# Two loads for the first half of x, LN1 sums shared out anew, and more transposes ahead of K, in a DiT block

## Chip, cores, metric

One core of a Trainium2 chip. The metric is the device time of one execution in microseconds, as the median of several runs; most runs of one kernel agree within 0.3%. Changes within 2% count as the same. TensorE runs the matmuls, VectorE, ScalarE and GpSimd the elementwise work, SyncE issues the loads.

## The reference

```python
B, N, D = 2, 256, 1152          # 512 tokens = 4 tiles of 128, two for each batch; 2 heads
mod = (silu(c) @ w_mod).reshape(B, 6, 1, D)      # shift_a, scale_a, gate_a, shift_m, scale_m, gate_m
h   = layernorm(x) * (1 + scale_a) + shift_a     # "LN1" below is this layernorm
q, k, v = h @ wqkv
a   = softmax(q k^T / sqrt(Dh)) v @ wo
x   = x + gate_a * a
h2  = layernorm(x) * (1 + scale_m) + shift_m
out = x + gate_m * (gelu(h2 @ w_fc1) @ w_fc2)    # all in bfloat16
```

## The kernel before

The kernel is a list of operations with dependencies. TensorE's and SyncE's order is the program's, the first part of VectorE's and ScalarE's is given in a list, and semaphores are set where an operation reads what another engine wrote. All weights pass once through one queue of loads. What the change touches is the first 20 us:

```python
# loads, in the order of SyncE's queue
for b in range(2):
    dma(X[:, 2*b:2*b+2, :], xv[b], ...)                  # x: tiles 0,1 then 2,3; 590 KB each, 4608 B a partition
for (ka, kb) in ((0, KC), (KC, KT)):                     # KC = 4, KT = 9
    for k0, k1 in ((0, 3), (3, 6), (6, 9)):
        dma(WSC[:, k0:k1, ka*P:kb*P], wmod_v[...], ...)  # scale_a's weights, 3 loads for each group of columns
    for kt in range(ka, kb):
        dma(WK[:, kt, :], wqkv_v[:, kt, D:2*D], ...)
...
# LN1: tiles 1, 2 by bn_stats on VectorE; tiles 0, 3 by two summing activations on ScalarE;
# the power -0.5 on GpSimd; xn_t = (x - mean) * rstd on VectorE
if t in (1, 2): ln_stats_dve(...)
else:           ln_stats_act(...)
...
# TensorE ahead of K (xn_T: nine 128x128 transposes of a tile, sca: two-column scale matmuls,
# warm: matmuls that only keep the clock up, hk: the scaled tile that K needs)
xn_T(1); warm(1); sca(0, 3); xn_T(0); warm(1); sca(3, 6); warm(1); sca(6, 9)
hk(0, 0); sc1a(0, KC); hk(1, 0); ...
xn_T(3, 0, 8)
k_first(0); k_first(1)                                   # 8 matmuls of 256 columns each: the K projection begins
xn_T(3, 8, 9); xn_T(2)                                   # ten transposes inside K's stream
...
for kt in range(KT):
    mod_kt(WSC, kt, 0, ..., (KC, KT))                    # 45 two-column matmuls, the second group of scales
hk(KC, 0); ...
k_pair(range(KC), 2, 1)                                  # 8 matmuls that cover hk(KC, 0)
...
# at the end, ahead of the last store: waits for the older stores, then for VectorE
```

## Time and profile before

| | before |
|---|---|
| time, median of 5 runs | 244.14 us (243.77 to 244.27) |
| TensorE busy | 238.2 us of a span of 243.0 |
| K's first matmul | 11.80 us |
| tiles 2, 3 of x in place | 5.99 us |

Times of landing, of single matmuls and of single packets are taken from the trace's records of semaphores, instructions and transfers; views of the profile merge them.

### The profile page before, as it was taken

What the parts mean: (1) busy time and instruction counts of PE and PEld (TensorE: products, weight loads), DVE (VectorE), ACT (ScalarE), POOL (GpSimd) and SP (SyncE); (2) the same over time, 40 slices, a digit from 0 to 9 for tenths busy, and PEclk for the clock granted to TensorE, in tenths of its full rate; (3) what the DMA queues carried; (4) which work ended last, traced back from release to release, by engine and by line L of the source; (5) the groups of instructions that cost most, each with busy time, mean ns of one, the idle gap of its engine ahead of it and who ended that gap; (6) DMA issues with size and microseconds to landing.
All of it is one profiled execution on the core that took longest, in us unless ns stands there. A gap on an engine that the chain in (4) does not pass through costs nothing.

```text
span 243.0 us, 4065 instructions
## 1 busy us (share of the span) xinstructions
PE 238.2 (98%) x1753; PEld 148.0 (61%) x1763; DVE 120.4 (50%) x217; ACT 67.2 (28%) x136; POOL 21.5 (9%) x39
## 2 busy tenths in 40 slices
PE   7999999999999999999999999999999999999996
PEld 2698854556667666898444444444656656666575
DVE  3724379596997899789999600000022222111112
ACT  4730350345424206983233322222000000000000
POOL 1500000000021186400000000020000000000000
DMA  6999999999995999979953498011000000000000
GB/s 237 334 381 392 392 391 391 398 414 405 389 350 170 350 386 393 392 266 392 323 162 82 166 308 323 0 32 68 0 16 19 16 16 19 16 16 19 18 28 21
DMA packets 30140, 51.59 MB, mean 212 GB/s; under 512 B 1703, under 2 KB 15787, under 8 KB 30123
## 3 DMA queue, kind: packets, MB, share of 16 engines
q1 hardware_dynamic: 29680, 50.14, 57.7%
q0 software_dynamic: 416, 1.19, 1.6%
q8 instruction: 14, 0.23, 0.4%
q14 instruction: 3, 0.02, 0.0%
q10 hardware_dynamic: 27, 0.00, 0.0%
HBM read 50.14 MB, written 1.19 MB: 211 GB/s over the span
## 4 chain that ended last, share of the span: by engine, by line
PE 94%; DMA 3%; SPq 1%; issue 0%; DVE 0%
PE psum L688 93%; DMA arena<-in_w_mod_dram 3%; PE psum L691 1%; SPq L669 1%; DVE arena L805 0%; DVE arena L1268 0%; DVE arena L1269 0%
## 5 line engine op out<-in xcount | busy, mean ns | idle before, releaser
L688 PE MATMUL psum<-arena 128*128 128x384 bf16 (+12 forms) x1664 | 234.8, 307 | 2.4 <-POOL arena L711 1.5
L688 PEld LDWEIGHTS psum<-arena 128*128 128x128 bf16 (+3 forms) x1674 | 142.7, 97 | 90.6 <-issue 4.5
L1063 DVE SCALAR_TENSOR_TENSOR arena<-arena 128x1152 f32<-128x1152 bf16 x32 | 44.7, 1414 | 0.6
L1268 DVE TENSOR_TENSOR arena<-psum,arena 128x384 f32<-128x384 f32 (+3 forms) x14 | 7.0, 501 | 68.0 <-PE psum L688 68.0
L1177 ACT ACTIVATE arena<-psum 128x512 bf16<-128x512 f32 (+1 forms) x44 | 22.4, 520 | 42.7 <-PE psum L688 42.7
L683 ACT ACTIVATE arena<-psum 128x512 bf16<-128x512 f32 (+6 forms) x37 | 19.6, 550 | 38.6 <-PE psum L688 37.0
L685 DVE CAST arena<-psum 128x512 bf16<-128x512 f32 (+3 forms) x13 | 8.2, 641 | 11.4 <-PE psum L688 11.3
L669 POOL DMA_DIRECT2D dit_scratch<-arena x3 | 1.8, 617 | 115.6 <-DVE arena L685 58.8
L1145 POOL TENSOR_TENSOR arena<-arena 128x384 f32<-128x384 f32 x12 | 10.9, 914 | 11.4 <-DVE arena L1144 9.8
L1090 DVE CAST arena<-psum 72x32 bf16<-72x32 f32 x1 | 0.2, 187 | 21.3 <-PE psum L688 21.3
L739 DVE BATCH_NORM_STATS2 arena<-arena 128x6 f32<-128x384 f32 (+1 forms) x18 | 9.5, 548 | 0.1
L1150 ACT ACTIVATE arena<-arena 128x1152 bf16<-128x1152 f32 x4 | 5.3, 1344 | 11.1 <-DVE arena L1149 11.1
L1144 DVE TENSOR_TENSOR arena<-psum,arena 128x384 f32<-128x384 f32 x12 | 6.5, 552 | 1.5 <-PE psum L688 0.9
L1269 DVE TENSOR_TENSOR arena<-arena 128x384 bf16<-128x384 f32 (+3 forms) x14 | 7.0, 501 | 0.5
L691 PE MATMUL psum<-arena 128*128 128x128 bf16 (+1 forms) x89 | 7.1, 219 | 0.0
L691 PEld LDWEIGHTS psum<-arena 128*128 128x128 bf16 (+1 forms) x89 | 5.8, 98 | 2.0 <-DMA arena<-in_c_dram 0.8
L1167 ACT ACTIVATE arena<-psum,arena 128x128 bf16<-128x128 bf16 x16 | 6.0, 456 | 1.7 <-PE psum L691 1.1
L1164 DVE TENSOR_SCALAR arena<-psum,arena 128x128 bf16<-128x128 bf16 x20 | 5.4, 336 | 1.9 <-PE psum L691 1.9
L1070 DVE TENSOR_REDUCE arena<-arena 128x36 f32<-128x1152 f32 x4 | 5.4, 1346 | 0.0
L1067 DVE STREAM_TRANSPOSE arena<-arena 128x1152 f32<-128x1152 f32 x4 | 5.4, 1363 | 0.0
L993 ACT ACTIVATE arena<-psum,arena 128x256 bf16<-128x256 f32 x8 | 3.7, 473 | 1.3 <-PE psum L688 0.9
L947 ACT ACTIVATE arena<-arena 128x256 bf16<-128x256 bf16 x6 | 2.6, 498 | 3.9 <-DVE arena L941 3.9
(48 smaller groups left out, 45.8 us busy)
## 6 DMA issues: line engine op xcount, KB each, us to landing
arena<-in_w_fc_dram SPq DMA_DIRECT2D x9, 1152.0 KB, 7.5
arena<-in_w_fc_dram SPq DMA_DIRECT2D x4, 2592.0 KB, 17.4
arena<-in_wqkv_dram SPq DMA_DIRECT2D x18, 288.0 KB, 10.3
arena<-in_w_mod_dram SPq DMA_DIRECT2D x3, 1728.0 KB, 20.4
arena<-in_w_mod_dram SPq DMA_DIRECT2D x3, 864.0 KB, 13.3
arena<-in_w_mod_dram SPq DMA_DIRECT2D x9, 288.0 KB, 10.8
arena<-in_wqkv_dram SPq DMA_DIRECT2D x1, 2592.0 KB, 16.7
arena<-in_wo_dram SPq DMA_DIRECT2D x1, 2592.0 KB, 24.4
```

Of the source, the lines that this page charges most:

```text
L683: act(c_act(n), lambda e: e.activation(out=dst, in_=src, func=ACTF.Copy), [src], [dst], name)
L685: dve(c_dve_psum16(n) if psum16 else c_dve_psum32(n), lambda e: e.tensor_copy(dst, src), [src], [dst], name)
L688: S.instr(lambda e: e.matmul(o, lhsT=l, rhs=r, start=st, stop=sp, **kw), reads=[l, r], writes=[o])
L691: S.instr(lambda e: e.transpose(o, i_, idn), reads=[i_, idn], writes=[o])
L739: dve(550, lambda e, s=s, o=o: e.bn_stats(out=o, in_=s), [s], [o], "bn_%s_%d" % (tag, ci))
L1063: dve(1270, lambda e, w=w, s=s, acc=acc: e.scalar_tensor_tensor(out=acc, in0=w, scalar=s, in1=acc, op0=ALU.mult, op1=ALU.add), [w, s, acc] ...
L1144: dve(550, lambda e, o=o, ga=ga, x1c=x1c: e.tensor_tensor(out=x1c, in0=o, in1=ga, op=ALU.mult), [o, ga], [x1c], "wo_t1_%d_%d" % (t, ci))
L1145: S.op("pool", 930, lambda e, xs=xs, x1c=x1c: e.tensor_tensor(out=x1c, in0=x1c, in1=xs, op=ALU.add), reads=[x1c, xs], writes=[x1c], name=" ...
L1167: act(440, lambda e, o=o, dst=dst, s1=s1, s2=s2: e.activation(out=dst, in_=o, func=ACTF.Identity, scale=s1, bias=s2), [o, s1, s2], [dst], ...
L1177: act(c_act(ntok), lambda e: e.activation(out=dst, in_=o, func=ACTF.Gelu_apprx_tanh), [o], [dst], "gelu_%d_%d" % (f, tok0))
L1268: dve(c_dve_psum32(w), lambda e, o=o, gm=gm, t1=t1: e.tensor_tensor(out=t1, in0=o, in1=gm, op=ALU.mult), [o, gm], [t1], "fc2_t1_%d_%d" % ( ...
L1269: dve(c_dve_32(w), lambda e, t1=t1, x1c=x1c, ost=ost: e.tensor_tensor(out=ost, in0=t1, in1=x1c, op=ALU.add), [t1, x1c], [ost], "fc2_out_%d ...
```

## The change

Its intent: ScalarE can begin LN1 when half of the first load is there, all but two of the transposes come before K begins so that K's stream carries two instead of ten, and half a K pair goes between the scale sums, which would otherwise wait for their last weights once K begins earlier.

```diff
-        for b in range(2):
-            dma(X[:, 2 * b:2 * b + 2, :], xv[b], ..., "ld_x%d" % b)
+        for t in (1, 0):
+            dma(X[:, t:t + 1, :], xv[0][:, t:t + 1, :], ..., "ld_x0_%d" % t, run=2304)
+        dma(X[:, 2:4, :], xv[1], ..., "ld_x1")
...
-        for i in range(5):          # warm-ups ahead of c's transpose
+        for i in range(3):
...
-            if t in (1, 2):         # statistics on VectorE
+            if t in (0, 2):
...
-        xn_T(1); warm(1, "c"); sca(0, 3); xn_T(0); warm(1, "d"); sca(3, 6); warm(1, "e"); sca(6, 9)
+        xn_T(1); xn_T(0); xn_T_copy(0, ...)
+        sca(0, 3); warm(1, ...); sca(3, 6); warm(2, ...)
+        xn_T(3, 0, 8); sca(6, 9); xn_T(2, 0, 8)
...
-        xn_T(3, 0, 8)
         k_first(0)
+        xn_T(3, 8, 9); xn_T(2, 8, 9)
         k_first(1)
-        xn_T(3, 8, 9); xn_T(2)
...
         for kt in range(KT):
+            if kt == 6:
+                k12(0)              # first half of the pair
             mod_kt(WSC, kt, 0, "scb_%d" % kt, (KC, KT))
...
-        k_pair(range(KC), 2, 1)
+        k12(1)                      # second half
...
# last store: the waits for older stores now come after the wait for VectorE in the program
```

The lines that set the orders of VectorE and ScalarE, and a subtraction that goes from VectorE to GpSimd, are cut.

## The prediction

> **What bounds the kernel now.** I read the page's busy shares first, then the chain of work that ended last.
>
> ```profile
> PE 238.2 (98%) x1753; PEld 148.0 (61%) x1763; DVE 120.4 (50%) x217; ACT 67.2 (28%) x136; POOL 21.5 (9%) x39
> ...
> GB/s 237 334 381 392 392 391 391 398 414 405 389 350 170 350 386 393 392 266 392 323 162 82 166 308 323 0 32 68 0 16 19 16 16 19 16 16 19 18 28 21
> ...
> PE 94%; DMA 3%; SPq 1%; issue 0%; DVE 0%
> ```
>
> TensorE is busy for 98% of the 243.0 us, and the chain is TensorE for 94% of them. So there are only two places where time can go: a gap in TensorE's stream, or TensorE work moved into otherwise empty time. The gaps are at the front. The same chain in order of time, from the first wait to the K projection:
>
> ```profile
> 2.87 7.88 DMA arena<-in_w_mod_dram
> 10.75 0.05 issue
> 10.79 0.47 PE psum L688 x12
> 11.26 0.14 PE psum L691 x2
> 11.39 0.36 DVE arena L805
> 11.75 0.05 issue
> 11.80 1.92 PE psum L688 x16
> 13.72 0.56 PE psum L691 x10
> 14.28 19.14 PE psum L688 x234
> ```
>
> Up to 10.75 us it is a transfer: the third scale load (part of w_mod), on a queue whose second slice of 6.1 us already moves 334 GB/s. Then 12 two-column scale matmuls, the first scaled tile hk_0_0 on VectorE (L805), and K's first matmul at 11.80. From there to the end the starts of successive matmuls, taken from the trace, show only pauses of about 0.1 to 0.25 us [...]. So 11.80 is the number that matters: **the end is K's start plus a fixed 231.2 us of stream**, and the ten transposes at 13.55 (x10) belong to that stream.
>
> The LN1 work that has to be ready by then, in the timelines of ScalarE, GpSimd and VectorE:
>
> ```profile
> 4.57 1.16 ACT L747 ACTIVATE arena<-arena 128x1152 bf16<-128x1152 bf16 x1 [0.41 <-DMA arena<-in_x_dram]
> ...
> 8.29 1.16 ACT L749 ACTIVATE arena<-arena 128x1152 bf16<-128x1152 bf16 x1
> ```
>
> ```profile
> 7.53 0.67 POOL L751 TENSOR_TENSOR arena<-arena 128x1 f32<-128x1 f32 x1
> ...
> 10.41 0.68 POOL L743 TENSOR_TENSOR arena<-arena 128x1 f32<-128x1 f32 x1
> ```
>
> ```profile
> 10.47 0.58 DVE L760 TENSOR_SCALAR arena<-arena 128x1152 bf16<-128x1152 bf16 x1 [0.61 <-POOL arena L751]
> 11.38 0.36 DVE L805 TENSOR_SCALAR arena<-psum 128x256 bf16<-128x256 bf16 x1 [0.33 <-PE psum L691]
> 11.66 0.16 DVE L795 COPY arena<-psum 128x8 f32<-128x8 f32 x1
> 11.85 0.35 DVE L805 TENSOR_SCALAR arena<-psum,arena 128x256 bf16<-128x256 bf16 x1
> 12.12 0.57 DVE L760 TENSOR_SCALAR arena<-arena 128x1152 bf16<-128x1152 bf16 x1
> ...
> 19.81 0.29 DVE L805 TENSOR_SCALAR arena<-arena,psum 128x256 bf16<-128x256 bf16 x1 [4.37 <-PE psum L688]
> ```
>
> L760 normalizes a token tile. Tile 3 is done at 11.05, tile 2 only at 12.69, after K has begun, which is why nine of its transposes sit inside the K stream.
>
> **What the Trainium skill says.** "TensorE: Matmul & The Clock Gate", "Wait — 56ns, not 53.3ns?": back-to-back 128-column matmuls start 55.6 ns apart when warm. The trace has its transposes 56 ns apart: it agrees. The same page, "The cost: per-tile semaphore tail": completion increments serialize, fitted at 26.3 ns each. In this trace the two-column matmuls start 26.6 ns apart, but their semaphore increments arrive 34.15 ns apart: the same mechanism, a larger figure. The lag grows by 7.55 ns per small matmul. The same page, "What's actually happening": the clock starts at half rate and rises after a busy window of some 3.4 us. Here 512-column warm-ups start 427 ns apart until about 6.6 us and 215 ns later. "DMA: Bandwidth & Descriptors", "Why small descriptors are slow (HBM only)": a fixed cost per packet, so an estimate of 2% more time at 2304 B than at 4608 B. The trace: 590 KB of x in 4608 B packets follow in 1.44 us (5.99 minus 4.55), 295 KB of wk in 2304 B packets in 0.75. So two halves cost 1.50, 0.06 more.
>
> **The change part by part.**
>
> *The load of x in two.* The bytes in front of the scale loads are the same; one more issue costs the queue 0.42 us on SyncE, but the scale loads land long after their issue (2.87 to 10.75), so only the packet size counts: the third scale load lands at about 10.80. Tile 1, 295 KB, should land near 3.65 instead of 4.55 (half of the 1.9 us in which the first load's packets ran).
>
> *Warm-ups 5 to 3.* The transpose of c waited at 3.75 behind the fifth warm-up, though c landed at 3.14. It moves to about 3.3, tanh (3.97 now) to 3.52, and ScalarE can begin on tile 1 at 3.75: 0.82 earlier than the 4.57 above.
>
> *LN1.* I shift the measured rows. ScalarE: sums of tile 1 at 3.75, of tile 3 at 6.20 (2.45 per tile, as from 4.57 to 7.02), after the second half of x at about 6.1. GpSimd follows with its present distances (the power for a ScalarE tile starts 2.96 after that tile's first sum): tile 1 at 6.71 to 7.38, then tile 0 to 7.95, tile 3 at 9.16 to 9.83, tile 2 after VectorE's statistics at 10.0 to 10.6. VectorE: tile 0's statistics from 4.65 to 6.6 (six instructions, 2.0 us now), one statistic of tile 2, xn_1 at 7.41, xn_0 at 7.98, the rest of tile 2's statistics to 9.95, xn_3 at 9.90 to 10.47, xn_2 at 10.63 to 11.2.
>
> *TensorE before K.* Transposes of tiles 1 and 0 at about 8.0 and 8.55; scales 0 to 5; two warm-ups; tile 3's eight transposes when xn_3 is done, 10.5 to 10.95; scales 6 to 8 from 10.95 instead of 10.79, ending at 11.27; tile 2's eight from 11.27 to 11.72. The signal of the last scale matmul came 0.27 after its start, hk_0_0 started at once, and K 0.414 after that. The same steps: 11.24 + 0.27 + 0.02 + 0.414 = **11.95, 0.15 later than 11.80**. The eight transposes hide behind hk_0_0.
>
> *The K stream.* Two transposes instead of ten: 8 x 0.056 = **0.45 less**.
>
> *The pair around the scale sums.* Now 45 small matmuls start 18.07 to 19.24, then a pair of 8 x 0.109 = 0.87 covers hk_4_0 (19.81 above) and K goes on at 20.16, with only 0.02 idle. The signal of the last small matmul came at 19.78, 0.54 after its start, of which 45 x 7.55 ns = 0.34 is the semaphore lag. With four wide matmuls after the 30th, the lag starts afresh: 15 x 7.55 ns = 0.11, so the signal comes after 0.31. But only four matmuls (0.44) are left to cover signal plus hk_4_0 and its release (0.35): 0.31 + 0.02 + 0.35 = 0.68 against 0.03 + 0.44. **Gap 0.21, so 0.19 more than now.** What the split is meant to save, a wait for the third load of this group, is not there: it lands at 18.53, its matmuls start at 18.87, and the stream is to come only about 0.3 earlier.
>
> *The last wait.* The last store now waits for the old stores after VectorE: two of those waits stand behind the VectorE one. In the compiled order of the new one the VectorE wait is the last, on the store itself. The trace has it released at 241.35 and issued at 241.43: **0.08 less**.
>
> Sum: +0.15 - 0.45 + 0.19 - 0.08 = -0.19 us, from 244.16 to **243.97**.
>
> **The rivals.** (a) *A floor at the scale load.* If xn_3 comes 0.2 us sooner than I reckon, K's start returns to the scale load's landing: 11.80 plus 0.05. The sum is then -0.29, and without the gap at the scale sums -0.48: 243.7. More is not possible while this load's order and bytes are the same. (b) *LN1 becomes the bound.* xn_3 now stands ahead of scales 6 to 8 on TensorE, and xn_2 ahead of hk_0_0 on VectorE; each 0.1 us that GpSimd's powers (0.57 to 0.68 each, two in a row at the end) come later moves K by nearly as much. 0.3 late makes 244.3. (c) *The clock rises later.* With three warm-ups TensorE idles from 2.8 to 3.3 before c. If the busy window then closes 2 us later, 18 transposes take 107 instead of 56 ns, the ScalarE copy that frees the bank for tile 3 slides from 9.3 to 10.0, and tile 3's last transposes wait to about 11.1: 244.4. Against it: the warm-ups are continuous from 3.4 on and the rise now comes at 6.6. (d) *No gap in the K stream:* 243.8.
>
> **Range and chances.** The floor in (a) limits the gain to about half a microsecond, 0.2%; (b) and (c) together cost hardly more. Runs before lie within 0.16 us. So 243.6 to 244.4. Two per cent would be 4.9 us, more than the whole change can touch: within 2% has 0.99.
>
> **What would show it.** In the new profile: the first sum on ScalarE near 3.75 instead of 4.57; xn_3 near 9.9 and xn_2 near 10.6; K's first 256-column matmul near 11.95; only two transposes after it; the first hk with a VectorE wait on TensorE after the scale sums followed by a TensorE gap near 0.2; the last store 0.08 closer to its VectorE release. It would be wrong if K started well before 11.8, which needs the scale load to land sooner, or if a new wait of over 0.5 us appeared between 12 and 34 us.

## More of the kernel before

One view that the prediction does not show matters later: the early stretches of the kernel before. The columns are the stretch, its length, the busy time of TensorE, its weight loads, VectorE, ScalarE and GpSimd (with instructions), the clock, the busy share of the transfer engines and GB/s.

```profile
1.75:3.75 2.00, 2.00 (x6) 0.46 (x4) 0.00 (x0) 0.96 (x1) 0.00 (x0) 1.00 0.92 320
3.75:5.75 2.00, 2.00 (x8) 0.86 (x8) 1.44 (x5) 1.37 (x3) 0.00 (x0) 1.00 0.97 356
5.75:7.75 2.00, 2.00 (x9) 0.79 (x7) 1.71 (x6) 1.97 (x4) 1.25 (x4) 1.00 0.95 285
```

x comes in at 320 to 356 GB/s without a break; from 5.75 us on, when mostly the scale weights in packets of 1024 bytes follow, it is 285.

## The result, and the profile after

| | before | after |
|---|---|---|
| time, median of 5 runs | 244.14 us (243.77 to 244.27) | 245.5 us (245.11 to 245.86) |
| tiles 2, 3 of x in place | 5.99 us | 7.70 us |
| third scale load in place | 10.75 us | 11.43 us |
| K's first matmul | 11.80 us | 13.39 us |

The ratio is 1.0057 (95% interval 1.0044 to 1.0071). The time is 1.1 us above the top of my range.

From the page of the changed kernel, the busy line and the chain by engine:

```profile
PE 238.3 (98%) x1752; PEld 147.7 (61%) x1762; DVE 120.3 (49%) x216; ACT 67.1 (27%) x136; POOL 21.2 (9%) x40
...
PE 94%; DMA 2%; ACT 1%; DVE 1%; issue 0%; SPq 0%; POOL 0%; POOLq 0%
```

TensorE's work is the same; ScalarE has come into the chain, and VectorE has a larger share of it (DVE was at 0%). In order of time it reads:

```profile
1.69 6.01 DMA arena<-in_x_dram
7.70 0.02 issue
7.72 1.26 ACT arena L748 x2
8.99 0.02 issue
9.01 1.26 ACT arena L750 x2
...
10.68 0.56 POOL arena L752
11.24 0.03 issue
11.27 0.59 DVE arena L761
11.86 0.05 issue
11.90 0.62 PE psum L691 x8
12.53 0.29 PE psum L688 x12
...
12.98 0.36 DVE arena L806
13.34 0.05 issue
13.39 1.05 PE psum L688 x8
...
14.54 6.62 PE psum L688 x95
21.17 0.29 DVE arena L806
21.46 0.05 issue
21.51 13.26 PE psum L688 x144
```

The head of the chain is no longer the scale load but the load of tiles 2, 3, issued at 1.69 and there at 7.70. ScalarE's two sums of tile 3 follow (L748, L750), its power on GpSimd (L752), its normalization on VectorE (L761, 11.27), eight transposes at 11.90, and only then the last 12 scale matmuls, though their load had been there since 11.43. K begins at 13.39. The hop over VectorE at 21.17 is the gap behind the scale sums that the prediction speaks of.

The same early stretches in the changed kernel:

```profile
1.75:3.75 2.00, 2.00 (x7) 0.56 (x6) 0.28 (x2) 1.16 (x3) 0.00 (x0) 1.00 0.91 292
3.75:5.75 2.00, 2.00 (x6) 0.76 (x5) 1.37 (x4) 1.97 (x3) 0.26 (x1) 1.00 0.83 208
5.75:7.75 2.00, 1.63 (x6) 0.35 (x3) 0.59 (x4) 0.55 (x3) 1.24 (x3) 1.00 0.95 326
```

From 3.75 to 5.75 us, just when tiles 2, 3 should come, the engines moved 208 GB/s instead of 356. They were busy 83% of the time, but single packets took very long: of those that began between 3 and 9 us, 15 took over 380 ns (the longest 1439), where 178 ns is usual for 4608 bytes. In the kernel before there were 2. A load is in place when the last of its 16 engines has delivered: for tiles 2, 3 they delivered from 5.25 to 5.99 us before, from 5.51 to 7.70 after. The first engines are on time; the stalled ones make the wait.

**The account.** The two traces can be cut at four marks:

| part | predicted | before | after | difference |
|---|---|---|---|---|
| to K's first matmul | +0.15 | 11.80 | 13.39 | +1.59 |
| from there to the first shift matmul | -0.45 + 0.19 = -0.26 | 17.63 | 17.39 | -0.24 |
| from there to the last matmul | 0 | 211.00 | 211.00 | 0.00 |
| last matmul to issue of the last store | -0.08 | 1.00 | 0.92 | -0.08 |
| issue of the last store to the end | 0 | 1.57 | 1.45 | -0.12 |

The sum is 1.15, the difference of the spans (244.15 less 243.00). The last row is scatter: over all undisturbed traces it runs from 1.45 to 1.99 us with no regard to the kernel. So the rows between came out as reckoned, and the first row has to be explained.

### The profile page after: what moved, and what is told of

Same layout as the page of the kernel before. It is cut to its first block, busy times and chain, and to the rows that moved or that the text cites. A ratio compares the mean times of both kernels' runs of the same rounds, so it can differ in the third digit from the quotient of the medians.

```text
span 244.2 us, 4065 instructions
## 1 busy us (share of the span) xinstructions
PE 238.3 (98%) x1752; PEld 147.7 (61%) x1762; DVE 120.3 (49%) x216; ACT 67.1 (27%) x136; POOL 21.2 (9%) x40
## 4 chain that ended last, share of the span: by engine, by line
PE 94%; DMA 2%; ACT 1%; DVE 1%; issue 0%; SPq 0%; POOL 0%; POOLq 0%
PE psum L688 92%; DMA arena<-in_x_dram 2%; PE psum L691 2%; ACT arena L750 1%; ACT arena L748 1%; SPq L669 0%; DVE arena L806 0%; DVE arena L761 0%; POOL arena L752 0%; DVE arena L1275 0%; DVE arena L1276 0%; POOL arena L751 0%; POOLq L473 0%
## 5 line engine op out<-in xcount | busy, mean ns | idle before, releaser
L688 PE MATMUL psum<-arena 128*128 128x384 bf16 (+11 forms) x1663 | 234.9, 307 | 3.2 <-POOL arena L712 1.5
L688 PEld LDWEIGHTS psum<-arena 128*128 128x128 bf16 (+4 forms) x1673 | 142.4, 97 | 91.2 <-issue 4.4
L685 DVE CAST arena<-psum 128x512 bf16<-128x512 f32 (+3 forms) x13 | 8.2, 641 | 11.4 <-PE psum L688 11.3
L1152 POOL TENSOR_TENSOR arena<-arena 128x384 f32<-128x384 f32 x12 | 10.9, 911 | 11.2 <-DVE arena L1151 9.7
```

What stands on the lines that cost most here:

```text
L685: dve(c_dve_psum16(n) if psum16 else c_dve_psum32(n), lambda e: e.tensor_copy(dst, src), [src], [dst], name)
L688: S.instr(lambda e: e.matmul(o, lhsT=l, rhs=r, start=st, stop=sp, **kw), reads=[l, r], writes=[o])
L1152: S.op("pool", 930, lambda e, xs=xs, x1c=x1c: e.tensor_tensor(out=x1c, in0=x1c, in1=xs, op=ALU.add), reads=[x1c, xs], writes=[x1c], name=" ...
```

## The experiments

Every run has a trace. The table puts them together by the loads of x in SyncE's queue ("590" and "295" are KB); the text below tells each. "Slow" counts packets over 380 ns between 3 and 9 us.

| run | base | loads of x ahead of the weights | slow | tiles 2, 3 in place | third scale load | K | ratio to before |
|---|---|---|---|---|---|---|---|
| before | | 590, 590 | 2 | 5.99 | 10.75 | 11.80 | 1 |
| e4 | before | 590, 590 | 7 | 6.03 | 10.68 | 11.73 | 0.9995 |
| e1 | after | 590, 590 | 1 | 6.18 | 10.62 | 12.88 | 1.0021 |
| after | | 295, 295, 590 | 15 | 7.70 | 11.43 | 13.39 | 1.0057 |
| e14 | after | 295, 295, 590 | 10 | 7.48 | 10.72 | 13.16 | 1.0011 |
| e2 | before | 295, 295, 590 | 13 | 6.82 | 11.44 | 12.49 | 1.0033 |
| e5 | before | 295, 295 (by rows), 590 | 13 | 8.74 | 11.86 | 13.33 | 1.0052 |
| e6 | after | 295, 295, 590 (small packets) | 15 | 7.99 | 11.62 | 13.67 | 1.0047 |
| e3 | after | 4 x 295 | 3 | 5.82 (3), 6.76 (2) | 10.71 | 12.06 | 1.0013 |
| e7 | after | 4 x 295 | 8 | 5.94 (3), 6.68 (2) | 10.83 | 12.01 | 1.0009 |
| e15 | after | 4 x 295 | 6 | 5.82 (3), 7.08 (2) | 10.74 | 12.13 | 0.9999 |
| e8 | after | 295, 295, 295, 295 (last two by rows) | 15 | 8.19 | 11.94 | 13.94 | 1.0088 |
| e9 | after | 295, 295, 590, tiny | 8 | 6.86 | 10.71 | 12.54 | 1.0034 |
| e10 | before | 590, 590, tiny | 10 | 5.79 | 11.17 | 12.22 | 1.0015 |
| e11 | after | 295, 295, 590, weights later | 14 | 6.92 | 10.68 | 12.60 | 1.0028 |
| e12 | before | 590, 295, 295 | 7 | 5.51 (3), 6.68 (2) | 11.03 | 12.08 | 0.9987 |
| e13 | after | 295, 590; one more on ScalarE's queue | 3 | 5.49 | 9.95 | 15.72 | 1.0116 |

### Is the late landing the cause?

**e0_after_again**: the changed kernel once more, no edit.

> The changed kernel once more, for what repeats. In its trace the second half of x (tiles 2, 3) landed at 7.70 us instead of 5.99, and K started at 13.39 instead of 11.80. Theory S (splitting the load of tiles 0, 1 itself slows the load behind it) and theory E (ScalarE's earlier sum, 3.73 instead of 4.57 us, slows the load it runs beside) both expect about the same again: x landed at 7 to 8 us, 245.5 us. Theory C (chance of one profile) expects 5.9 to 6.2 us in this trace.

Measured: 245.35 to 245.77 us in its undisturbed runs, ratio 1.0045. The profiled execution was a disturbed one of 702 us, and its trace is not used. The slower time repeats; on the landing this run says nothing.

**e1_x_one_load**

```diff
-        for t in (1, 0):
-            dma(X[:, t:t + 1, :], xv[0][:, t:t + 1, :], ...)
-        dma(X[:, 2:4, :], xv[1], ...)
+        for b in range(2):
+            dma(X[:, 2 * b:2 * b + 2, :], xv[b], ...)
```

> The changed kernel with tiles 0, 1 of x in one load again. S and E: tiles 2, 3 land at about 6.0 us as in the kernel before, ScalarE's first sum starts at 4.57 as there. Then by the rows of before: ScalarE ends tile 3 at 9.55, its power at 10.65, tile 2's power at 11.3, tile 2 normalized at 11.9, its transposes to 12.4, K near 12.45: 0.65 later than before, less 0.45 for eight transposes out of the K stream, 0.08 at the end, plus 0.2 at the scale sums: about 244.45 us. C expects no difference to the changed kernel but that by ScalarE's later start.

Measured: tiles 2, 3 at 6.18 us, K at 12.88, 244.99 us, ratio 1.0021. ScalarE's timeline in this run:

```profile
4.79 1.16 ACT L747 ACTIVATE arena<-arena 128x1152 bf16<-128x1152 bf16 x1 [1.22 <-DMA arena<-in_x_dram]
...
7.24 1.15 ACT L747 ACTIVATE arena<-arena 128x1152 bf16<-128x1152 bf16 x1
```

The second sum no longer waits for a load: it follows the first tile's work. Without the split the late landing is gone, and half of the slowdown with it; the other half fits with this order of LN1 needing the early start that the split was to give: in the chain to K, LN1's steps follow each other from the landing at 4.77 us on. K is 0.43 later than I reckoned, 0.22 of it because the first load itself came at 4.77 instead of 4.55.

**e2_x_split_only**: the kernel before with the two lines of the split.

> The kernel before with nothing but the load of tiles 0, 1 split as in the change. Here VectorE takes tile 1 and ScalarE tile 0, so ScalarE starts no earlier than at about 4.45 us. S: tiles 2, 3 land late all the same, 7 to 8 us, the third scale load near 11.4 instead of 10.75, K near 12.4, about 244.8 us. E: tiles 2, 3 land at about 6.1 us, K within 0.1 of 11.80, 244.1 to 244.2 us.

Measured: tiles 2, 3 at 6.82, the third scale load at 11.44, K at 12.49, 245.4 us, ratio 1.0033. The split alone makes the kernel slower, with ScalarE starting at 4.41 us: theory E, that ScalarE's earlier work disturbs the load, fails as the whole cause. The landing itself is short of the 7 to 8 us that theory S expected; the third scale load and K are as S expected. Here another load is late too; among TensorE's waits from 8.5 to 25 us stands

```profile
PE psum L688 <- DMA arena<-in_w_mod_dram: 0.8, 2, 0.4
```

The two are the scale loads of both groups, and the stretch from K to the shift matmuls is 18.15 us instead of 17.63.

**e3_x_four_loads**

```diff
-        for t in (1, 0):
-            dma(X[:, t:t + 1, :], xv[0][:, t:t + 1, :], ...)
-        dma(X[:, 2:4, :], xv[1], ...)
+        for t in (1, 0, 3, 2):
+            dma(X[:, t:t + 1, :], xv[t // 2][:, t % 2:t % 2 + 1, :], ...)
```

> The changed kernel with tiles 3 and 2 in two loads as well, so that all of x comes in packets of 2304 bytes. If S acts through the step from 2304-byte to 4608-byte packets, both land at about the time of before (5.3 and 6.1 us) and the result is my predicted 243.9 to 244.1. If it acts through the number of loads, or if E holds, they land late, tile 2 at 7 us or later, and the time is 245 or more.

Measured: tile 3 at 5.82 us, tile 2 at 6.76, K at 12.06; 244.73 us where before is 244.57, ratio 1.0013 (0.9995 to 1.0031). That is above the 243.9 to 244.1 that I expected, 0.4 of it because the kernel before is higher on this chip too (244.57). The stretch in question, and ScalarE's two first sums:

```profile
3.75:5.75 2.00, 2.00 (x7) 0.60 (x5) 1.41 (x4) 1.97 (x3) 0.26 (x1) 1.00 0.95 329
```

```profile
3.75 1.16 ACT L747 ACTIVATE arena<-arena 128x1152 bf16<-128x1152 bf16 x1 [0.39 <-DMA arena<-in_x_dram]
...
6.20 1.15 ACT L747 ACTIVATE arena<-arena 128x1152 bf16<-128x1152 bf16 x1
```

With tile 3 in time, the sums begin at 3.75 and 6.20, to the hundredth what I had reckoned for the changed kernel, tile 3 is normalized at 9.94 (reckoned 9.90) and K begins at 12.06 (11.95). So the late landing accounts for 1.33 of the 1.59 us in the first row of the account, 0.15 was reckoned, and my steps behind the landing hold to 0.11. (Tile 2 runs close behind: its power ends at 10.93 and it is normalized at 10.96, reckoned 10.6 and 10.63, so that its eight transposes end just before K. That is the second half of rival (b).) **e15_four_loads_again** repeats it:

> The kernel with four loads of x, unchanged: its scatter. Tile 3 at 5.7 to 6.0 us, tile 2 at 6.6 to 6.9, K at 11.9 to 12.2, 244.4 to 245.0 us; a tile 3 after 6.5 us would say that the two traces so far were luck.

Measured: 5.82, 7.08 and K at 12.13; 244.63 us, ratio 0.9999. **e14_after_third** does so for the changed kernel:

> The changed kernel, unchanged: its scatter. All theories but chance: tiles 2, 3 between 6.8 and 7.8 us, K between 12.5 and 13.5, 245.1 to 245.9 us.

Measured: 7.48 and K at 13.16; its two runs were 245.46 (the profiled one) and 244.39 us, the second below what I expected. In this trace 15 of the 16 engines had delivered by 5.94 us and a single one held the load until 7.48. The late landing repeats; its size scatters.

### Does the split of the K pair cost what I said?

**e7_four_loads_pair_whole**: e3 with

```diff
-            if kt == 6:
-                k12(0)
...
-        k12(1)
+        k_pair(range(KC), 2, 1)
```

> The changed kernel with x in four loads and the K pair whole behind the 45 scale matmuls, as before the change. My account: the gap of 0.23 us behind the scale sums goes down to 0.02; K at about 12.05, the Q projection 0.2 earlier than in the kernel with four loads (33.48), near 33.28, and 0.2 us less in time: 244.5 where before is 244.57. Against it: if the wait for the third of the second scale loads comes into the gap's place, Q stays at 33.4 to 33.5 and the time at 244.7.

Measured: 17.39 us from K to the shift matmuls, the same as in e3; ratio 1.0009. The gap of 0.23 us behind the scale sums is gone (0.02 is left), but the chain shows what took its place:

```profile
8.16 10.65 DMA arena<-in_w_mod_dram
18.81 0.05 issue
18.86 2.21 PE psum L688 x30
```

The third load of the second group lands at 18.81 in this trace, and the last 15 scale matmuls wait 0.23 us for it. So in this trace the split would have traded one wait for an equal one. It is one trace, and the landing scatters: in e3 and e15 the same load was there at 18.09 and 18.14, and the 31st sum of e7 was due at 18.63, so with such a landing the whole pair would have waited for nothing. That the wait "is not there" was true of the changed kernel, where the sums come 1.1 us later and the load landed at 18.75; with K as early as I predicted it can come, and what the split costs or saves there is not shown.

The sign that I had named, an earlier Q projection (33.22 against 33.48), says nothing: the trace of e3 lacks the record of Q's first matmul. It has 1752 matmuls where e7 has 1762, and the first of Q that it has starts 325 ns after the matmul before it, which is 109 and one missing matmul of 216. The traces of before and of the changed kernel lack ten each against e4 and e14, the same kernels. So of the pauses that the prediction saw behind K, those of 0.22 us are missing records; the cause of those of 0.1 us is not shown.

### Why does the load land late?

**e4_before_again**: the kernel before, for a second trace.

> The kernel before, unchanged, for a second trace of it. In its first trace two packets behind 3 us took over 380 ns, against 15 in the changed kernel, 12 with the split alone and 3 with four loads of x. Theory C (chance) expects counts up to 10 here too; theories P and N (below) expect at most 4, tiles 2, 3 at 5.9 to 6.3 us and K at 11.7 to 12.0.

Measured: 7 slow packets (more than 4, so the count alone is a weak mark), landing at 6.03, K at 11.73. **e5_x_halves_by_rows**, in the kernel before:

```diff
-        for b in range(2):
-            dma(X[:, 2 * b:2 * b + 2, :], xv[b], ...)
+        for p0 in (0, 64):
+            dma(X[p0:p0 + 64, 0:2, :], xv[0][p0:p0 + 64], ...)
+        dma(X[:, 2:4, :], xv[1], ...)
```

> The kernel before with tiles 0, 1 of x loaded in two halves by partitions (0 to 63, 64 to 127), 4608-byte packets throughout. Theory N (three loads of x instead of two, one more issue ahead of the weights, makes the packets behind slow) expects over ten packets above 380 ns behind 3 us, tiles 2, 3 at 7 us or later, K at 12.3 or later. Theory P (a load in 4608-byte packets behind loads in 2304-byte packets does it) expects at most 4 such packets, tiles 2, 3 at about 6.1 us and the time of before, 244.2 to 244.6.

Measured: 8.74 us, K at 13.33, ratio 1.0052, with packets of 4608 bytes throughout. But here the halves are slow themselves: they land at 4.64 and 6.00 us, where the halves by tiles of the changed kernel land at 3.71 and 4.43. **e6_x1_small_packets**, in the changed kernel:

```diff
-        X = sb(O_X, 9216).rearrange("p (t d) -> p t d", t=4)
+        # the same bytes, tiles in the order 0, 2, 1, 3: tiles 2, 3 are two runs of 2304 bytes in each partition
```

> The changed kernel with the tiles of x laid out in the on-chip memory in the order 0, 2, 1, 3, so that tiles 2, 3, still one load, come in 2304-byte packets like the others. P: at most 4 slow packets, tiles 2, 3 at 6.0 to 6.7 us, K at 12.0 to 12.3, 244.4 to 244.9 us, near the kernel with four loads (244.73). N: slow as in the changed kernel, tiles 2, 3 after 7 us, 245.5 us.

Measured: 7.99 us, ratio 1.0047, with packets of 2304 bytes throughout. Theory P, a step in packet size, fails on both, and on e6 without that doubt. **e8_x1_by_rows**, in the changed kernel:

```diff
-        dma(X[:, 2:4, :], xv[1], ...)
+        for p0 in (0, 64):
+            dma(X[p0:p0 + 64, 2:4, :], xv[1][p0:p0 + 64], ...)
```

> The changed kernel with tiles 2, 3 loaded in two halves by partitions, 4608-byte packets: four loads of x of 295 KB, as in the kernel with four loads, but with the step in packet size. So far three loads of x were late four times out of four, two and four never. Theory L (a load of 590 KB behind two of 295 KB is what stalls) and theory M (three loads bad, four good, whatever their size) both expect the last of tiles 2, 3 at 6.7 us, K near 12.05 and 244.7 us. If it is late (over 7 us, K over 12.6) then the four loads owed their good time to the packets of 2304 bytes alone.

Measured: 8.19 us and K at 13.94, the worst of the landings but one, with four loads of 295 KB. M (three loads bad, four good) and L (the big third load is what stalls) both expected 6.7. But the loads by rows were slow in e5 from the first on, so a trouble of their own is not ruled out, and e8 alone does not refute M and L. **e9_tiny_fourth** and **e10_tiny_third** add to the changed kernel and to the kernel before, behind the loads of x:

```diff
+        dma(TINY, xv[0][:, 0, 0:2], P * 4, "ld_tiny")
```

> The changed kernel with a fourth load of 4 bytes for each partition behind the three of x, ahead of the weights. M, or a theory by which the time of issue of the first weight load matters (T: 2.16 us in the changed kernel, 2.64 with four loads), expects tiles 2, 3 at 6.0 to 6.5 us and K near 12.1. L expects tiles 2, 3 still after 7 us and K at 13 or later.

> The kernel before with the same load of 4 bytes for each partition behind its two of x. M and T expect what three loads showed: tiles 2, 3 (or the weights just behind) with over ten packets above 380 ns and the third scale load at 11.4 us or later instead of 10.7. L expects no difference to the kernel before: tiles 2, 3 at 6.0, the third scale load at 10.6 to 10.9 us.

Measured: e9 lies between (6.86, K at 12.54): later than M expected with four loads (6.0 to 6.5), earlier than L did (after 7). In e10 x is in time (5.79), but ten slow packets, eight of them of the weights behind, put the third scale load at 11.17 and K at 12.22. L expected none of this (10.6 to 10.9 for that load), M somewhat more (11.4 or later). **e11_weights_later**, in the changed kernel:

```diff
+        by["ld_sc0_0"].instrs[0].deps.update(by["c_half"].instrs)
```

> The changed kernel, its three loads as they are, but the first weight load is issued only after VectorE's first use of c (about 3.65 us instead of 2.16). Theory W (issuing the weights' loads while x moves is what stalls the third load of x) expects tiles 2, 3 at 5.5 to 6.2 us; the third scale load then at about 11, K near 12.2, 244.8 us or less. L and M expect tiles 2, 3 after 7 us as before, K at 13.3 or later, 245.5 us or more.

Measured: the weights are issued from 3.73 us on, the landing is at 6.92, K at 12.60. Better than the changed kernel and between what W (5.5 to 6.2) and L and M (after 7) expected, but 14 slow packets are left: the weights' issue is not all that makes them. **e12_second_split**, in the kernel before:

```diff
-            dma(X[:, 2:4, :], xv[1], ...)
+        for t in (3, 2):
+            dma(X[:, t:t + 1, :], xv[1][:, t - 2:t - 1, :], ...)
```

> The kernel before with tiles 0, 1 in one load as there and tiles 3, 2 in two: three loads of x, but the split is in the second place. Theory F (it is the split of the first load that hurts: the engines reach the third load early, while little is queued) expects tiles 2, 3 by 6.3 us, the third scale load at 10.6 to 10.9, K at 11.7 to 12.0. Theory N (any third load) expects the last of them after 6.7 us or the third scale load after 11.1, K at 12.2 or later.

Measured: 6.68 for the last tile, 11.03 for the third scale load, K at 12.08: between what F and N expect, nearer to N. The time is 244.33 against 244.68, unclear (0.996 to 1.0014). **e13_tile1_on_act_queue**, in the changed kernel:

```diff
-        for t in (1, 0):
-            dma(X[:, t:t + 1, :], ...)
+        dma(X[:, 1:2, :], xv[0][:, 1:2, :], ..., eng="act")
+        dma(X[:, 0:1, :], xv[0][:, 0:1, :], ...)
...          # the load's place in ScalarE's list, and one semaphore more
```

> The changed kernel with the load of tile 1 issued from ScalarE, behind that of c, so that SyncE's queue has two loads of x as in the kernel before. If the late landing comes from three x loads in one queue (N, F): tiles 2, 3 at 5.8 to 6.3 us, the third scale load by 10.8, K at 11.9 to 12.2, 244.0 to 244.5 us where before is 244.3. If it comes from splitting in whatever queue: tiles 2, 3 after 6.7 us, K at 12.5 or later, 244.9 us or more.

Measured: tiles 2, 3 at 5.49 us and the third scale load at 9.95, 0.8 earlier than in the kernel before, with 3 slow packets: SyncE's queue with two loads of x was in order. But tile 1, on the other queue, came only at 5.9 us, TensorE stood idle, and its clock fell:

```profile
6.47 1.92 PE L688 MATMUL psum<-arena 128*128 128x512 bf16 x6
10.60 1.95 PE L691 MATMUL psum<-arena 128*128 128x128 bf16 x18 [2.21 <-DVE arena L761]
```

The first transposes still start 55 to 69 ns apart, those from 10.85 us on 107 instead of 56. K began at 15.72, ratio 1.0116: the landing was as hoped, the time as feared for another reason. The clock is the smaller part of it: three runs had a mean clock of 0.993 and took 247.85 to 248.01 us, and the fourth, at 1.0, took 246.58, still 1.9 above the kernel before (244.68).

**What follows.** In the four traces with two loads of x in SyncE's queue and nothing more ahead of the weights (before, e4, e1, e13), tiles 2, 3 were in place by 6.2 us and the third scale load by 10.75. In every trace with more, one of the two was later: the last of x at 6.7 to 8.7 us, or (e10) the scale load. In the split that I study the loss sits in packets that take up to 1.4 us, from about 4 us on. That much is shown. Which property of the additional loads makes single packets wait is open. A step in packet size (e6), ScalarE's work beside it (e2) and the weights' issue (e11) have each failed as the sole cause; a big load behind small ones did so in e10, which has none; against the number three there are only e8, with its doubt, and e9, which lies between. Most versions have one trace, and traces of like loads (after and e14 against e2, e9, e11) scatter by 0.9 us.

None of the versions is shown to beat the kernel before: e3, e7 and e15 reach it within 0.13%, and e12's 0.9987 is within its scatter.

## Why the prediction was wrong

"Within 2%" was right; the time and the range were not. By its own steps:

- **The load of x in two: wrong, and nearly the whole error.** The step that failed reads "the scale loads land long after their issue (2.87 to 10.75), so only the packet size counts", with "the second half of x at about 6.1" by the same reckoning. I treated the queue as a pipe that moves bytes at one rate whatever they are cut into. The measured landing was 7.70, so the sum of tile 3 began at 7.72 instead of 6.20. From there to K I had 5.75 us (6.20 to 11.95); the trace has 5.67. Of the signs that I named, xn_3 (11.27 for 9.9), xn_2 (11.92 for 10.6) and K (13.39 for 11.95) show it; the landing itself I had not named.
- **The early start: right.** ScalarE began at 3.73 (reckoned 3.75), since tile 1 landed at 3.71 (3.65). But K does not hang on tile 1. The time won there ends in a wait of 1.45 us before tile 3's sum.
- **Ten transposes to two, and the gap behind the scale sums: right.** Together -0.24, reckoned -0.26. The gap was 0.23 (reckoned 0.21); hk_4_0 started 0.341 after the last scale matmul's start (reckoned 0.31 + 0.02), against 0.57 before, as the lag of the semaphore increments demands. That the split saved no wait was partly luck: it held in the changed kernel, whose K came 1.4 us later than I had it, and not in e7.
- **The last wait: right.** -0.08.
- **The rivals.** Rival (b) named the bound that came, LN1 of tile 3 ahead of the scale matmuls, but only GpSimd's powers as its reason, with 0.1 to 0.3 us. No rival let the transfer itself get slower, and so the range ended at 244.4. It was too narrow even for the rivals that I had: (b) at 0.3 us and (c), 244.4 by itself, together give 244.7. Rival (c), a clock that rises later, did not come in the changed kernel (the first warm-up at 217 ns started at 6.79 us, 6.74 before); in e13 transposes ran at 107 ns, since the clock had fallen again.
- **Was the gain real otherwise?** With tile 3 in time (e3, e15) K is 0.26 to 0.33 later than before instead of 0.15, which the -0.24 and the -0.08 just pay for.

## What to carry to other kernels

A load cut in two was not the same stream in smaller pieces here: look at the landing of the load behind it, not only at that of the first half, and give the range room for it when the chain begins with a transfer. Work moved ahead of a critical stage ties that stage to more inputs; ask for each of them what it does if it is a microsecond late. When the other terms are right to 0.1 us and the total is off by 1.5, cut the traces at a few marks before thinking about causes.

## What the Trainium skill lacked or had wrong

- "TensorE: Matmul & The Clock Gate", "The cost: per-tile semaphore tail", fits 26.3 ns for each serialized increment and 4.7 more for each tile, 31.0 where every matmul has one. Here increments of two-column matmuls arrive 34.15 ns apart while the matmuls start 26.6 ns apart; the lag, 0.34 us after 45 of them, was worth 0.2 us at a hand-over to VectorE.
- The same page, "What's actually happening", has the clock fall after an idle window of some 3.4 us. In e13 about 2.2 us without a matmul (8.39 to 10.60 us) came before it: the next four gaps were still 55 to 69 ns, those from 10.85 us on 107. The 3.4 us that ended with this fall held some 1.2 us of matmuls, an estimate from these starts and ends. The rise came between 4.8 and 7.7 us over the traces, 3.3 to 6.2 us after the first warm-up, for nearly the same stream of warm-ups.
- "DMA: Bandwidth & Descriptors" prices a transfer by its bytes, its packets and a fixed cost. No section that I found tells that one more load ahead in the same queue can slow the packets of the next: 208 GB/s instead of 356 over 2 us, packets of up to 1439 ns where 178 is usual.
- No page that I read gives the scatter of a last store: 1.45 to 1.99 us from its issue to the end in the traces.
